# Fused attention and mixture of experts on one core: where the first expert's weights are split into two parts

## The chip, the core and the metric

The kernel runs on one core of a Trainium2 chip. A core has five engines that work side by side, each through its own queue, in order: TensorE (PE in the profile; its weight loads are PEld), VectorE (DVE), ScalarE (ACT), GpSimd (POOL) and SyncE (SP), which here only issues DMA transfers. Tiles lie in SBUF, matmul results in PSUM. The metric is the device time of one execution in microseconds (us).

## The reference

q, k and v have shape [8 batches, 8 heads, 576 rows, 64]. Keys and values are averaged over 8 neighbouring rows, so that each head has 72 of them. Then come softmax attention and a layer of 8 experts in which each of the 4608 tokens goes to the one with the largest logit:

```python
k_p = k.reshape(B, H, Sp, pool, D).mean(axis=3)          # v_p likewise
scores = scale * np.matmul(q, k_p.transpose(0, 1, 3, 2))
attn = softmax(scores); x = np.matmul(attn, v_p)         # -> x [4608, 512]
logits = x @ w_gate;  expert_idx = argmax(logits)        # gate_w: its probability
h = np.maximum(xe @ w1[e], 0.0);  ye = h @ w2[e]         # per expert, w1 512x1024
out[mask] = gate_w[mask, None] * ye
```

All inputs and outputs are float32.

## The kernel before, in words

**Two sections.** `attention` computes x, picks the expert of every token and scatters the rows into a table in DRAM (`dispatched`), sorted by expert. `experts` reads the table back in units of up to 512 rows and multiplies them with the weights of their expert. Between them stands the transition: the last routing, the first matmuls of expert 0, and `plan`, a chain of small VectorE operations that lays out the units. `experts` begins with a critical section (line 728): every engine enters it once the work ahead of it is done.

**Weights in two parts.** TensorE multiplies in a reduced float32 format (fp32r). To keep accuracy, each weight is held as a high part (the cast to fp32r) and a low part (the weight less its high part), in the tile `W` of four planes: w1 high, w1 low, w2 high, w2 low. The weights of one expert come in eight pieces of 128 x 1024 numbers (512 KB): 0 to 3 are w1, 4 to 7 are w2. To split a piece takes a cast on ScalarE (line 424) and a subtraction on VectorE or GpSimd (line 425). The first expert's pieces are loaded (`w_load`, line 418) and split (`w_split`) inside the attention loop, the other experts' in the experts' section.

**The attention loop.** 36 tiles t of 128 rows, four groups of nine, two batches per group. The queues follow the order in which the code is written (no planner moves instructions). In step t: transposes of the probabilities P of tile t on TensorE (line 283) and their copies `pt` out of PSUM on ScalarE (284); scores of tile t+2 (263), their row maxima and the subtraction `sd` on VectorE (267, 270); transposes of q for t+3 (253); at some t a transpose of pooled keys and values of the next group (180) or an expansion of V (207); the exponential of t+2 on ScalarE (276); P times V of tile t (`weigh`, 299); and on VectorE the division by the row sums (311 to 315). Sums of neighbouring rows of k and v (`kv_pool`, 172) run on VectorE, woven in between, and on GpSimd at t = 0 to 2 and then 3, 6, 9, 12, 15 and 18.

**Routing.** Tiles are routed in batches of three (the last two batches have two and one). When a batch is complete, VectorE picks each row's expert (374 to 379, `ro` at 346). In the next step, after `scale`, TensorE counts (356, 359), VectorE reads the counts (361, 362), and GpSimd multiplies (`rp`, 388) and copies the tokens' numbers (384); this falls on every t that is a multiple of 3. A further sum on VectorE (389) needs `rp`; after it GpSimd scatters the three tiles (368, 407). `x_load` (436, 437) at t=29 reads 512 rows of expert 0 back; `x_split` (453 to 456) splits them from t=32 on.

**The first expert's pieces before.** Piece i is loaded in step 18 + i and split in step 21 + i, after everything else of the step: the cast always on ScalarE, the subtraction on GpSimd for i = 0, 3, 6 (t = 21, 24, 27), on VectorE for the other five (t = 22, 23, 25, 26, 28). A piece lies in one of four slots that also take the raw keys and values (`kraw`), so a load waits on SyncE until the slot's last reader is through.

**The transition before.** `multiply` issues the first expert's w1 products for hidden rows 0 to 5 in portions, `hidden(f)` takes row f out of PSUM: a ScalarE activation (468) and a VectorE subtraction (469). `more_hidden` stands inside `plan`, `last_hidden` behind it. The w2 planes are first read after the entry to `experts` (line 882).

**Tiles.** The pooled keys `kTs` have twice the needed columns: each of the two heads that share 128 partitions has its own 72 columns, and the rows of the other head there are zero. Two memsets write the zeros: one on VectorE before anything else (line 101), one on GpSimd (493). The scores read only the 64 rows and 72 columns of their head.

Of the kernel before, what the change touches and what calls it, by code (L numbers as in the profile page):

```python
# [10 lines left out]
F32 = mybir.dt.float32  # L11
# [28 lines left out]
COPIED = 2  # L40
W0T = 21
AHEAD = 8
# [36 lines left out]
def attention(ctx, outer, tc, q, k, v, wg, w1v, w2v, xs, W, cst, carry, tab, banks):  # L79
# [10 lines left out]

    kTs = [one.tile([P, 2, 4, 2 * SK], F32, name=f"kT{i}") for i in range(2)]
    kvp = e1.tile([P, NT, P], F32, name="kvp")
# [7 lines left out]
    nc.vector.memset(kvp, 0.0)  # L100
    nc.vector.memset(kTs[0], 0.0)
    nc.vector.memset(vT, 0.0)
# [73 lines left out]
    def kv_transpose(g, i, bank, what="kv", take=nc.scalar.copy):  # L176


        for c in range(3):
            nc.tensor.transpose(bank[:, c * P : (c + 1) * P], kvp[:, 3 * i + c, :], ident)  # L180
        m = bank[:, 0 : 3 * P].rearrange("p (c bj hp k) -> p hp bj k c", c=3, hp=2, k=8)
        for hp in range(2):
            rk, rv = slice(64 * hp, 64 * hp + 64), slice(64 - 64 * hp, 128 - 64 * hp)
            ko = kTs[g % 2].rearrange("p b j (hp k c) -> p hp (b j) k c", hp=2, c=9)
            vo = vT[:, 0 : 2 * H * KP].rearrange("p (bj hp x) -> p hp bj x", hp=2, x=KP)[:, :, :, 0:SK].rearrange("p hp b (k c) -> p hp b k c", c=9)
            if "k" in what:
                take(out=ko[rk, hp, :, :, 3 * i : 3 * i + 3], in_=m[0:64, hp])
            if "v" in what:
                take(out=vo[rv, hp, :, :, 3 * i : 3 * i + 3], in_=m[64:128, hp])
# [67 lines left out]
    def scores(t):  # L257
        g = t // NT
        for j in range(4):
            for p0, b in [(0, 0), (64, 1)] if KIND(t) == 4 else [(0, parts(t)[0][2]), (64, parts(t)[0][2])]:  # L260
                for hp in range(2):
                    r = slice(64 * hp, 64 * hp + 64)
                    nc.tensor.matmul(pS[p0 : p0 + 64, hp, j * SK : (j + 1) * SK], lhsT=qT[t][r, j * P + p0 : j * P + p0 + 64],  # L263
                                     rhs=kTs[g % 2][r, b, j, hp * SK : (hp + 1) * SK], start=True, stop=True, skip_group_check=True)
        s4 = pS[:, :, 0:288].rearrange("p a (h x) -> p a h x", h=4)
# [149 lines left out]
    def w_load(i):  # L415

        raw = kraw.tile([P, 1024], F32, tag="raw", name=f"w0_{i}")
        nc.sync.dma_start(out=raw.rearrange("p (c f) -> p c f", c=4 if i < 4 else 2), in_=load_piece(w1v, w2v, 0, i))
        w0[i] = raw

    def w_split(i):
        raw = w0.pop(i)
        c, a = slice((i % 4) * 1024, (i % 4 + 1) * 1024), 0 if i < 4 else 2
        nc.scalar.copy(out=W[:, a, c], in_=raw)
        (nc.gpsimd if (W0T + i) % NB == 0 else nc.vector).tensor_tensor(out=W[:, a + 1, c], in0=raw, in1=f32(W[:, a, c]), op=ALU.subtract)

# [15 lines left out]
    def x_open():  # L444
        early.close()
        m1 = outer.enter_context(tc.tile_pool(name="m1", bufs=1, side="right", reuse_waits="tile"))
        u0["H"] = m1.tile([P, 2, 8, 512], F32R, name="H")
        u0["X"] = m1.tile([P, 2, 4, 512], F32R, name="X")

    def x_split(s):  # L450
# [41 lines left out]
    sums()  # L492
    nc.gpsimd.memset(kTs[1], 0.0)

# [48 lines left out]
    for t in range(total):  # L543
# [14 lines left out]
        for at, n, *gj in adds:  # L558
            if at == t:
# [4 lines left out]
                del pieces[third][:n]  # L564
        if 0 <= t - W0T + 3 < 8:
            w_load(t - W0T + 3)
        if 0 < t < total - 2:
# [43 lines left out]
        for bt, (t0, nb) in enumerate(batches):  # L611
            if t == t0 + nb - 1:
                route(bt)
        if 0 <= t - W0T < 8:
            w_split(t - W0T)
        if t == total - 7:
# [23 lines left out]
    def more_hidden():  # L640
        hidden(1)
        multiply(12)

    def last_hidden():
        for f in range(2, AF_EV):
            hidden(f)
            multiply(12)

# [877 lines left out]
```

## Time and profile before

| | |
|---|---|
| median of 3 runs | 631.41 us (631.15 to 631.75) |
| the profiled execution's own time | 627.27 us |
| its span | 625.7 us |
| mean granted clock of TensorE | 0.998 |
| busy: PE, DVE, ACT, POOL | 599.4, 347.9, 241.4, 241.7 us |
| attention loop, transition, entry to the experts | to 171, to 187, at 189 us |
| casts of the first expert's pieces (line 424) | 8, mean 1.04 us |
| subtractions on VectorE and on GpSimd (line 425) | 5 of 1.22 us, 3 of 2.36 us |

The profile is of one execution; its times are microseconds from the span's start. A row of a timeline shows start, duration, engine, line, operation, output <- inputs, and in brackets the idle time before it and what ended it. A row of a group shows busy time and mean duration in ns. A row of waits shows who waited for whom, in total, how often, and the longest. The chain of waits is the work that ended last, followed backwards. A busy TensorE is not TensorE at its peak: its instructions are pipelined, and their ends are modelled.

### The profile page before, as it was taken

The page shows a single profiled execution, that of the slowest core. Times are in us where ns is not written, and L with a number is a line of the kernel's source. Part 1 is how long each engine was busy: PE and PEld are TensorE (multiplying, and loading weights), DVE is VectorE, ACT ScalarE, POOL GpSimd, SP SyncE. Part 2 cuts the span into 40 slices and gives each one's busy share as a digit, 9 for nine tenths or more (in the row PEclk, how much of TensorE's full clock was granted, in tenths as well). Part 3 has the DMA queues.
Part 4 walks back from the last instruction along what each step waited for, and adds up shares of the span by engine and source line. Part 5 has one row for each costly group of instructions (what it writes and reads, how often), then busy time and mean ns, then how long its engine had stood idle before and what let it go on. Part 6 is the DMA issues. An engine that isn't in the chain of part 4 may idle for free.

```text
span 625.7 us, 13480 instructions
## 1 busy us (share of the span) xinstructions
PE 599.4 (96%) x4412; PEld 511.0 (82%) x4412; DVE 347.9 (56%) x731; ACT 241.4 (39%) x453; POOL 241.7 (39%) x288
## 2 busy tenths in 40 slices
PE   6989999999999999999999999999999999999995
PEld 5778989888877878789897888888898888888994
DVE  6699898888751324368475532755137764133220
ACT  2567776877411114065363411523024641021110
POOL 7447657644321122367444411152116861101101
PEclk9999999999999999999999999999999999999999
DMA  9999998982334931506967853064304353100001
GB/s 321 367 279 267 306 262 263 252 253 70 126 111 145 288 112 54 186 25 179 289 185 230 273 115 87 2 211 136 105 35 143 89 146 71 56 0 37 36 4 53
DMA packets 93938, 96.48 MB, mean 154 GB/s; under 512 B 43102, under 2 KB 74846, under 8 KB 93792
## 3 DMA queue, kind: packets, MB, share of 16 engines
q1 hardware_dynamic: 85808, 74.27, 42.3%
q0 software_dynamic: 7440, 20.50, 9.2%
q8 instruction: 61, 1.00, 0.7%
q14 instruction: 85, 0.70, 0.4%
q10 hardware_dynamic: 544, 0.02, 0.0%
HBM read 72.68 MB, written 26.00 MB: 158 GB/s over the span
## 4 chain that ended last, share of the span: by engine, by line
PE 76%; DVE 9%; issue 5%; POOL 4%; ACT 2%; DMA 2%; DVEq 0%; SPq 0%; ACTq 0%; POOLq 0%
PE pU L882 32%; PE pP L860 20%; PE pq L860 10%; PE pU L299 4%; DMA XE<-in_v_dram 2%; PE pP L283 2%; PE pP L463 2%; POOL dispatched L407 2%; PE pS L263 1%; PE pq L253 1%; DVE raw L172 1%; DVE mx L267 1%; POOL raw L172 1%; PE pm L207 1%; DVE xe L315 1%
## 5 line engine op out<-in xcount | busy, mean ns | idle before, releaser
L882 PE MATMUL pU<-W,H 128*128 128x512 f32 x912 | 216.3, 397 | 0.0
L882 PEld LDWEIGHTS pU<-W,H 128*128 128x128 f32 x912 | 171.3, 188 | 41.0
L860 PE MATMUL pP<-X,W 128*128 128x512 f32 (+3 forms) x748 | 143.2, 345 | 4.2 <-DVE W L1069 1.5
L860 PEld LDWEIGHTS pP<-X,W 128*128 128x128 f32 x748 | 122.7, 188 | 21.4 <-issue 3.0
L1351 POOL DMA_INDIRECT out_dram<-Y,GT x51 | 52.8, 1036 | 192.5 <-DVE Y L1174 179.3
L1069 POOL TENSOR_TENSOR W<-ST,W 128x1024 fp32r<-128x1024 f32 x30 | 77.8, 2607 | 88.1 <-ACT W L1061 88.1
L971 ACT ACTIVATE H<-pP 128x512 fp32r<-128x512 f32 (+1 forms) x67 | 36.0, 538 | 191.0 <-PE pP L860 154.7
L1174 DVE TENSOR_SCALAR Y<-pU,GT 128x512 f32<-128x512 f32 x36 | 27.0, 749 | 107.6 <-PE pU L882 106.2
L992 DVE SCALAR_TENSOR_TENSOR H<-pP,H 128x512 fp32r<-128x512 f32 (+2 forms) x73 | 42.2, 580 | 72.0 <-ACT H L971 70.3
L860 PE MATMUL pq<-X,W 128*128 128x512 f32 (+3 forms) x364 | 73.0, 348 | 2.4 <-issue 1.7
L860 PEld LDWEIGHTS pq<-X,W 128*128 128x128 f32 x364 | 60.0, 188 | 11.7 <-issue 2.5
L1061 ACT CAST W<-ST 128x1024 fp32r<-128x1024 f32 x56 | 57.3, 1054 | 6.7 <-DMA ST<-in_moe_w_dram 6.7
L299 PE MATMUL pU<-V,pt 110*128 110x146 f32 (+3 forms) x468 | 56.7, 283 | 1.4 <-ACT pt L284 0.8
L299 PEld LDWEIGHTS pU<-V,pt 110*128 110x128 f32 (+3 forms) x468 | 51.4, 179 | 3.1 <-ACT pt L284 1.8
L407 POOL DMA_INDIRECT dispatched<-xe,ix x36 | 39.8, 1107 | 18.2 <-POOL ix L368 9.8
L971 ACT ACTIVATE H<-pq 128x512 fp32r<-128x512 f32 (+1 forms) x33 | 17.9, 542 | 70.0 <-PE pq L860 68.5
L1069 DVE TENSOR_TENSOR W<-ST,W 128x1024 fp32r<-128x1024 f32 x26 | 40.5, 1560 | 4.6 <-ACT W L1061 4.1
L992 DVE SCALAR_TENSOR_TENSOR H<-pq,H 128x512 fp32r<-128x512 f32 (+2 forms) x35 | 20.8, 595 | 30.6 <-ACT H L971 29.8
L284 ACT COPY pt<-pP 110x384 f32<-110x384 f32 x72 | 30.9, 481 | 6.5 <-PE pP L283 5.8
L1049 DVE TENSOR_TENSOR X<-pS,X 128x512 fp32r<-128x512 f32 x34 | 21.9, 685 | 19.0 <-ACT X L1034 11.3
L276 ACT ACTIVATE P<-sd 128x576 f32<-128x576 f32 x36 | 24.8, 689 | 19.9 <-DVE sd L270 18.0
L172 POOL TENSOR_TENSOR raw<-raw 128x768 f32<-128x768 f32 (+1 forms) x18 | 26.3, 1460 | 13.5 <-DMA raw<-in_v_dram 12.8
(185 smaller groups left out, 625.4 us busy)
## 6 DMA issues: line engine op xcount, KB each, us to landing
ST<-in_moe_w_dram SPq DMA_DIRECT2D x56, 512.0 KB, 6.3
raw<-in_k_dram SPq DMA_DIRECT2D x12, 768.0 KB, 7.3
raw<-in_v_dram SPq DMA_DIRECT2D x11, 768.0 KB, 10.1
XE<-dispatched SPq DMA_DIRECT2D x104, 64.0 KB, 2.5
qa<-in_q_dram SPq DMA_DIRECT2D x24, 256.0 KB, 7.5
w<-in_moe_w_dram SPq DMA_DIRECT2D x8, 512.0 KB, 5.3
XE<-dispatched SPq DMA_DIRECT2D x15, 256.0 KB, 4.3
qa<-in_q_dram SPq DMA_DIRECT2D x2, 1024.0 KB
```

What stands on the lines that cost most here:

```text
L172: return lambda: eng.tensor_tensor(out=out, in0=raw[:, :, 0:n], in1=raw[:, :, n : 2 * n], op=ALU.add)
L284: take(out=pt[t][a][0:R], in_=pPs[a][0:R, 0 : 3 * P])
L299: nc.tensor.matmul(pu[p0 : p0 + n, a, h * VW : (h + m) * VW], lhsT=pt[t][a][0:r, c % 3 * P + p0 : c % 3 * P + p0 + n], rhs=Vs[g % 2][0:r, ...
L407: apart(nc.gpsimd.indirect_dma_start(out=xs, out_offset=bass.IndirectOffsetOnAxis(ap=at, axis=0), in_=rows, in_offset=None))
L860: r = pe.matmul(out=pH[g % 3][:, :m], lhsT=w1s(w, f, k), rhs=x, start=i == 0, stop=i == len(passes) - 1)
L882: r = pe.matmul(out=pY[:, s % 2, :], lhsT=h, rhs=w[:, k * 512 : (k + 1) * 512], start=start and i == 0, stop=stop and i == len(ps) - 1, sk ...
L971: act.activation(out=HH[:, f, o], in_=src[:, o], func=AF.Relu).then_inc(Q["A_h"], 1)
L992: return dve.scalar_tensor_tensor(out=dst[:, f, to], in0=src[:, at], scalar=0.0, in1=f32(HH[:, f, at]), op0=ALU.max, op1=ALU.subtract)
L1061: act.copy(out=(W1H if i < 4 else W2H)[:, o], in_=ST[:, i, :]).then_inc(Q["A_s1" if i < 4 else "A_s2"], 1)
L1069: eng.tensor_tensor(out=(W1L if i < 4 else W2L)[:, o], in0=ST[:, i, :], in1=f32((W1H if i < 4 else W2H)[:, o]), op=ALU.subtract).then_inc( ...
L1174: r = dve.tensor_scalar(out=Y[:, s, :], in0=a, scalar1=gate, scalar2=None, op0=ALU.mult)
L1351: pool.indirect_dma_start(out=out, out_offset=bass.IndirectOffsetOnAxis(ap=GT[:, u, s, 1:2].bitcast(I32), axis=0), in_=Y[:, s, :], in_offs ...
```

## The change

- The pieces 0 to 4 are split at t = 18, 21, 24, 27 and 30, all five subtractions on GpSimd. They are loaded three steps ahead, at t = 15, 18, 21, 24 and 27.
- The pieces 5 to 7 are loaded at t = 32, 33 and 34 into a new tile `late` (12 KB per partition), which lies beside `H` and `X` in the memory that the early pools have given back at t = 31. They are split in the transition: the cast of piece 5 follows hidden row 1 inside `plan`, those of 6 and 7 follow hidden row 2; VectorE subtracts 5 and 6 after hidden row 2 and 7 after hidden row 3.
- The key tiles have half their columns, one set of 72 for both heads of a pair; the two memsets are gone.

```diff
-W0T = 21
+W0T = (18, 21, 24, 27, 30)
@@
-    kTs = [one.tile([P, 2, 4, 2 * SK], F32, name=f"kT{i}") for i in range(2)]
+    kTs = [one.tile([P, 2, 4, SK], F32, name=f"kT{i}") for i in range(2)]
@@
-    nc.vector.memset(kTs[0], 0.0)
@@
-            ko = kTs[g % 2].rearrange("p b j (hp k c) -> p hp (b j) k c", hp=2, c=9)
+            ko = kTs[g % 2].rearrange("p b j (k c) -> p (b j) k c", c=9)
@@
-                take(out=ko[rk, hp, :, :, 3 * i : 3 * i + 3], in_=m[0:64, hp])
+                take(out=ko[rk, :, :, 3 * i : 3 * i + 3], in_=m[0:64, hp])
@@ scores
-                                     rhs=kTs[g % 2][r, b, j, hp * SK : (hp + 1) * SK], ...
+                                     rhs=kTs[g % 2][r, b, j, :], ...
@@ w_load
-        raw = kraw.tile([P, 1024], F32, tag="raw", name=f"w0_{i}")
+        raw = kraw.tile([P, 1024], F32, tag="raw", name=f"w0_{i}") if i < len(W0T) else u0["late"][:, i - len(W0T)]
@@
-    def w_split(i):
-        raw = w0.pop(i)
+    def w_high(i):
+        nc.scalar.copy(out=W[:, 0 if i < 4 else 2, (i % 4) * 1024 : (i % 4 + 1) * 1024], in_=w0[i])
+
+    def w_low(i, eng):
         c, a = slice((i % 4) * 1024, (i % 4 + 1) * 1024), 0 if i < 4 else 2
-        nc.scalar.copy(out=W[:, a, c], in_=raw)
-        (nc.gpsimd if (W0T + i) % NB == 0 else nc.vector).tensor_tensor(out=W[:, a + 1, c], in0=raw, in1=f32(W[:, a, c]), op=ALU.subtract)
+        eng.tensor_tensor(out=W[:, a + 1, c], in0=w0.pop(i), in1=f32(W[:, a, c]), op=ALU.subtract)
@@ x_open
+        u0["late"] = m1.tile([P, 8 - len(W0T), 1024], F32, name="late")
@@
-    nc.gpsimd.memset(kTs[1], 0.0)
@@ the loop
-        if 0 <= t - W0T + 3 < 8:
-            w_load(t - W0T + 3)
+        if t + 3 in W0T:
+            w_load(W0T.index(t + 3))
+        if 32 <= t < 40 - len(W0T):
+            w_load(t - 32 + len(W0T))
@@
-        if 0 <= t - W0T < 8:
-            w_split(t - W0T)
+        if t in W0T:
+            w_high(W0T.index(t))
+            w_low(W0T.index(t), nc.gpsimd)
@@ more_hidden
         hidden(1)
+        w_high(5)
         multiply(12)
@@ last_hidden
             hidden(f)
+            if f == 2:
+                w_high(6)
+                w_high(7)
+            for i in ((5, 6), (7,))[f - 2]:
+                w_low(i, vec)
             multiply(12)
```

More of the change, by code (lines that the diff above doesn't have):

```diff
@@ L263, in scores @@
                     nc.tensor.matmul(pS[p0 : p0 + 64, hp, j * SK : (j + 1) * SK], lhsT=qT[t][r, j * P + p0 : j * P + p0 + 64],
-                                     rhs=kTs[g % 2][r, b, j, hp * SK : (hp + 1) * SK], start=True, stop=True, skip_group_check=True)
+                                     rhs=kTs[g % 2][r, b, j, :], start=True, stop=True, skip_group_check=True)
         s4 = pS[:, :, 0:288].rearrange("p a (h x) -> p a h x", h=4)
```

## The prediction

> **What bounds the kernel now.** First the page: the whole span, and the chain that ended last.
>
> ```profile
> span 625.7 us, 13480 instructions
> PE 76%; DVE 9%; issue 5%; POOL 4%; ACT 2%; DMA 2%; DVEq 0%; SPq 0%; ACTq 0%; POOLq 0%
> w<-in_moe_w_dram SPq DMA_DIRECT2D x8, 512.0 KB, 5.3
> ```
>
> TensorE carries three quarters of the chain, VectorE 9%. The last row is the load of one piece of the first expert's weights: 5.3 us from issue to landing. Where VectorE's share touches this change is seen in the chain between 104 and 172 us (columns: start, duration, engine, tile, line), and the price of a piece in the groups kept apart by shape (busy, mean ns).
>
> ```profile
> 120.40 1.04 ACT W L424
> 121.46 1.23 DVE W L425
> 125.94 1.22 DVE W L425
> 138.73 1.22 DVE W L425
> ...
> L424 ACT CAST W<-w 128x1024 fp32r<-128x1024 f32 x8 | 8.3, 1036 | 0.0
> L425 POOL TENSOR_TENSOR W<-w,W 128x1024 fp32r<-128x1024 f32 x3 | 7.1, 2360 | 0.8 <-ACT W L424 0.8
> L425 DVE TENSOR_TENSOR W<-w,W 128x1024 fp32r<-128x1024 f32 x5 | 6.1, 1220 | 0.7 <-ACT W L424 0.7
> ```
>
> A piece costs a cast of 1.04 us on ScalarE and a subtraction of 1.22 us on VectorE or 2.36 us on GpSimd. Three of the five subtractions on VectorE (tiles t=22, 23, 26) lie on the chain; those of t=25 and 28 do not, nor do the three on GpSimd (t=21, 24, 27). So this change is worth what TensorE loses between tiles 22 and 31, not 5 x 1.22 us.
>
> **What the loop gives back.** TensorE's own order, each row the start of a tile's transposes of P (t=22, 23, 29, 30, 31), and from the chain a key/value transpose and an expansion of V:
>
> ```profile
> 115.24 0.84 PE L283 MATMUL pP<-ident,P 128*110 128x128 f32 x6
> 119.59 0.87 PE L283 MATMUL pP<-ident,P 128*110 128x128 f32 x6
> 126.42 1.71 PE L299 MATMUL pU<-V,pt 110*128 110x146 f32 x12 [0.81 <-ACT pt L284]
> 145.39 0.82 PE L283 MATMUL pP<-ident,P 128*110 128x128 f32 x6
> 148.74 0.82 PE L283 MATMUL pP<-ident,P 128*110 128x128 f32 x6
> 152.26 0.84 PE L283 MATMUL pP<-ident,P 128*110 128x128 f32 x6
> ...
> 110.17 0.33 PE pm L180 x3
> 134.67 0.68 PE pm L207 x6
> ```
>
> Tile 29 has no extra work and takes 148.74 - 145.39 = 3.35 us; tile 30, with a batch's counts, 3.52, so counts cost 0.17. Tiles 22 to 30 take 152.26 - 115.24 = 37.02. Their work is 9 x 3.35, two transposes (0.66), four expansions (2.72), three counts (0.51): 34.04. So 2.98 is lost. Of it tile 22 loses 119.59 - 115.24 - 3.35 - 0.33 = 0.67, before any split on VectorE and beside the cast of t=21, which stays. 2.31 is the most that can come back. The least is the one wait that a row names behind t=23's cast and subtraction, 0.81. I take **2.1**: nearer the upper end, because TensorE sits at its work in tiles 29 and 30, and the casts at t=24 and 27 that stay have an expansion of 0.68 in the following tile beside them, which lets TensorE work while the copies of P wait.
>
> **What the new places cost.** At t=18 GpSimd also adds a chunk of V. Rows of GpSimd, VectorE and TensorE there, and two from the start of the kernel:
>
> ```profile
> 108.92 0.59 POOL L172 TENSOR_TENSOR kvp<-raw 128x192 f32<-128x192 f32 x1
> 117.47 0.22 POOL L388 TENSOR_TENSOR rp<-rp,ro 128x24 f32<-128x24 f32 x1 [3.11 <-DVE rp L361]
> ...
> 111.12 0.95 DVE L172 TENSOR_TENSOR raw<-raw 128x768 f32<-128x768 f32 x1
> 114.74 0.18 DVE L346 TENSOR_TENSOR ro<-rk,rn 128x24 bf16<-128x24 f32 x1
> 115.14 0.18 PE L356 MATMUL pm<-ro,lstrict 128*128 128x24 bf16 x1
> 118.29 0.76 DVE L270 TENSOR_TENSOR sd<-pS,mx 128x576 f32<-128x576 f32 x1
> ...
> 30.20 1.82 POOL L172 TENSOR_TENSOR raw<-raw 128x768 f32<-128x768 f32 x1 [3.24 <-DMA raw<-in_v_dram]
> 30.67 2.17 DVE L172 TENSOR_TENSOR raw<-raw 128x768 f32<-128x768 f32 x1
> ```
>
> The split follows the add at 109.51 and runs to 111.87. Its scatters come 2.36 later; the 3.11 of idle time before the next batch's work covers that (uncovered, VectorE's next sum would wait for `rp`). But VectorE's add at 111.12 now meets it. The last pair shows such a meeting: beside GpSimd's add the same VectorE add took 2.17 instead of 0.95, and ended 0.82 after the other. So this one ends at about 112.7 instead of 112.07. VectorE has no idle time from there to `ro`, which ends at 115.5 to 115.6 instead of 114.92; the counts on TensorE wait for it, at 115.14 before. Cost **0.5** (0 if the add slips by, 0.75 if the whole rest of the split is waited for and no slack is left). The 118.29 row lies inside GpSimd's split of t=21 (117.80 to 120.16) and has its usual 0.76, so not every VectorE instruction waits.
>
> The Trainium skill (SBUF — State Buffer, "Who interferes with whom") draws that line: a VectorE instruction with two SBUF inputs contends with a GpSimd one that reads SBUF, the later one waits until the first is done, and one with a PSUM input doesn't contend. By it the meeting at t=18 is the only one, at 0.75. Were every VectorE instruction held instead, the two pieces new to GpSimd (t=18, 30) would cost up to 2 x 2.36, which the 118.29 row speaks against.
>
> ScalarE's cast at t=18 lies beside an expansion (tile 19), as at t=27: nothing. At t=30 the next tile has none:
>
> ```profile
> 146.57 1.22 DVE L425 TENSOR_TENSOR W<-w,W 128x1024 fp32r<-128x1024 f32 x1
> ...
> 152.87 0.69 ACT L276 ACTIVATE P<-sd 128x576 f32<-128x576 f32 x1 [1.43 <-DVE sd L270]
> 153.57 0.84 ACT L284 COPY pt<-pP 110x384 f32<-110x384 f32 x2
> 154.28 1.48 PE L299 MATMUL pU<-V,pt 110*64 110x146 f32 x24
> 162.01 1.02 POOL L407 DMA_INDIRECT dispatched<-xe,ix  x1 [6.19 <-DVE lh L313]
> ```
>
> The cast of 1.04 goes ahead of the two copies; the first is then done at 154.61 + 0.42 = 155.03, and the matmuls that began at 154.28 wait 0.75. VectorE hands `sd` over some 0.3 earlier, since t=28's subtraction is gone from in front of it: **0.45** (0 to 0.75). GpSimd's part costs nothing there: its scatter waits until 162.01 anyway.
>
> **What is moved behind the loop.** ScalarE, VectorE and TensorE in the transition, SyncE's last load before it, what SyncE waits for at the experts' entry (total, times, longest), and two rows on the order of accesses to W:
>
> ```profile
> 157.28 1.12 SPq L437 DMA_DIRECT2D GT<-dispatched  x1
> 178.90 0.60 ACT L468 ACTIVATE H<-pq 128x512 fp32r<-128x512 f32 x1 [2.20 <-PE pq L463]
> 180.13 0.69 DVE L469 SCALAR_TENSOR_TENSOR H<-pq,H 128x512 fp32r<-128x512 f32 x1
> 182.33 0.69 DVE L469 SCALAR_TENSOR_TENSOR H<-pP,H 128x512 fp32r<-128x512 f32 x1 [1.51 <-ACT H L468]
> 188.76 5.87 PE L860 MATMUL pP<-X,W 128*128 128x512 f32 x24 [1.50 <-DVEq L1400]
> ...
> SPq L728 <- PE pq L463: 4.2, 1, 4.2
> ...
> 143.49 2.36 POOL L425 TENSOR_TENSOR W<-w,W 128x1024 fp32r<-128x1024 f32 x1 [0.40 <-ACT W L424]
> 145.48 1.06 ACT L424 CAST W<-w 128x1024 fp32r<-128x1024 f32 x1
> ```
>
> The three late loads go out behind 158.40, the first lands near 163.7; its cast must be done by hidden row 2 at 178.90, so begin by 177.86: 14 us of cover. The last pair shows ScalarE writing one piece of W while GpSimd still reads another, so a late cast should not wait for the matmuls on the other pieces. The casts of pieces 6 and 7 run from 179.50 to 181.58. VectorE does hidden row 2 until 180.82, two subtractions until 183.26, hidden row 3 until 183.95, the third until 185.17. TensorE ends at 188.76 - 1.50 = 187.26, and the entry waits for it last (4.2 us behind VectorE). 185.17 lies 2.1 us ahead of that: **0**; without that cover, one for one.
>
> The smaller rest also costs 0. The memsets of the key tiles end before data are there:
>
> ```profile
> 5.74 1.55 DVE L172 TENSOR_TENSOR raw<-raw 128x768 f32<-128x768 f32 x2 [0.31 <-DMA raw<-in_k_dram]
> ```
>
> VectorE stands idle 0.31 for the first keys with its memset, and would stand longer without. Scores read the same 72 columns. On SyncE the first piece now goes ahead of a chunk of V and the others further back among the loads of q; no wait of the loop between 80 and 165 us ends with a load, so one piece's 5.3 us at most is absorbed (uncovered, GpSimd's add of V would be late by as much).
>
> **Sum**: -2.1 + 0.5 + 0.45 = -1.15 us. The profiled execution took 627.27 (span 625.7 and 1.6 around it), so 626.1; the runs' median is 631.41, 4.1 above it, and the difference carries over: **630.3**. A difference under 0.2% (1.26 us) cannot be told from none here.
>
> **The rivals.**
> - *Both costs vanish*: the add slips past the split and the cast is covered. Then -2.1 to -2.3, **629.2**. For it: VectorE's earlier hand-over, estimated and not seen. Against: the pair at 30.20.
> - *Nothing is left, the change doesn't pay*: only 0.81 comes back and the costs stand at 0.75 each: +0.7, **632.1**. For it: one wait alone is named. Against: 2.31 us lost in the tiles.
> - *The entry waits for the late splits*. The late tile lies partly where the raw keys and values lay. Suppose its loads are held until 178.9: piece 5 lands at 184.2; its cast (185.24) stands ahead of hidden row 2 on ScalarE (185.84), which stands ahead of VectorE's share (186.53), two subtractions (188.97), hidden row 3 (189.66) and the third subtraction (190.88). The entry comes 3.6 later than at 187.26: +3.6 - 1.15 = +2.45, **633.9**, slower. It decides from a landing of piece 5 at 180.6 on; from 181.7 on the kernel is slower than before. For it: three in-order queues must fit. Against: 14 us of cover, and GpSimd's split of t=30, the last reader of that place, is over some 3 us after its cast.
>
> **How the numbers follow.** Forecast 0.46, costs vanish 0.22, nothing left 0.20, entry 0.12. The forecast's own range is 629.6 to 631.1, so it lies on both sides of the 0.2% line at 630.15: 0.17 of it counts as faster. Faster 0.22 + 0.17 = 0.39, same 0.29 + 0.20 = 0.49, slower 0.12. The range goes from the full 2.3 without costs, less 0.3 for the spread of the runs (628.8), to the second rival (632.2), and leaves out part of the last.
>
> **What would show it.** Tiles 24 to 30 at 3.35 plus their extras, with no wait behind `ro` or ScalarE's copies: the 2.1. A VectorE add of more than 1.5 us beside GpSimd's split at t=18: the 0.5. A wait of TensorE at tile 31 for the copies: the 0.45. At the entry, TensorE still the last that SyncE waits for. Wrong would be a VectorE or DMA wait there, or a gain over 2.3 us.

## The result

| kernel | median | lowest to highest | runs |
|---|---|---|---|
| before | 631.75 us | 631.15 to 634.95 | 5 |
| changed | 637.61 us | 635.00 to 639.06 | 5 |

The ratio is 1.0065 with a 95% interval of 1.0040 to 1.0091: slower, by 0.65% or some 4 us (the medians are 5.9 us apart), where 1.15 us of gain were forecast. The page of the changed kernel's profiled execution (637.93 us), its span and the shares of its chain:

```profile
span 636.3 us, 13472 instructions
...
PE 77%; DVE 7%; issue 6%; POOL 5%; DMA 2%; ACT 1%; DVEq 0%; SPq 0%; ACTq 0%; POOLq 0%
```

VectorE's share of the chain fell from 9% to 7%, as the change means it to; "issue", GpSimd and TensorE have 1% more each, and the span grew by 10.6 us. As will be seen, the two profiled executions belong to two kinds that differ without any change of the kernel, so these two pages must not be subtracted. First the rows that answer the forecast's steps. The transition, on VectorE and TensorE (start, duration, engine, line, operation):

```profile
189.17 2.35 DVE L425 TENSOR_TENSOR W<-late,W 128x1024 fp32r<-128x1024 f32 x2
192.04 1.22 DVE L425 TENSOR_TENSOR W<-late,W 128x1024 fp32r<-128x1024 f32 x1
...
192.74 2.96 PE L462 MATMUL pq<-X,W 128*128 128x512 f32 x12
197.26 1.91 PE L867 MATMUL pP<-X,W 128*128 128x512 f32 x7 [1.56 <-DVEq L1407]
```

The three late subtractions end at 193.26; TensorE ends its hidden rows at 195.70 and begins the experts 1.56 later, against 1.50 before. The moved pieces cost nothing there. Then tile 20 and what follows, GpSimd, VectorE, TensorE and ScalarE:

```profile
113.83 2.36 POOL L425 TENSOR_TENSOR W<-w,W 128x1024 fp32r<-128x1024 f32 x1
117.33 1.03 POOL L406 DMA_INDIRECT dispatched<-xe,ix  x1 [0.28 <-POOL ix L367]
118.84 0.96 POOL L406 DMA_INDIRECT dispatched<-xe,ix  x1 [0.28 <-issue]
...
115.40 1.61 DVE L171 TENSOR_TENSOR raw<-raw 128x768 f32<-128x768 f32 x1
119.50 0.76 DVE L266 TENSOR_REDUCE mx<-pS 128x8 f32<-128x576 f32 x1 [0.61 <-PE pq L252]
...
116.81 0.73 PE L262 MATMUL pS<-kT,qT 64*64 64x72 f32 x32
120.61 0.17 PE L355 MATMUL pm<-ro,lstrict 128*128 128x24 bf16 x1 [0.80 <-DVE mx L266]
...
120.22 0.59 ACT L254 COPY qT<-pq 128x512 f32<-128x512 f32 x1 [2.36 <-PE pU L298]
```

VectorE's add beside GpSimd's split took 1.61, as forecast. But there is something that no row of the kernel before had shown. TensorE's scores end at 117.54, and the maximum over them starts at 119.50, ScalarE's copy of the next q at 120.22 after 2.36 of idle time. TensorE's results were there; the news of them was not. It came while GpSimd went through its scatters (at 117.33, 118.84 and 120.28): for the maximum 1.1 after the first had ended, for the copy 0.4 after the second.

This can be measured over the loop from the trace's semaphore events. TensorE's semaphore is the counter that tells the other engines that a group of matmuls is done. For each group that raises it, take the time from the end of its last matmul to the next raise that the trace records, between 45 and 172 us. In this trace the mean is 0.63 us for the 47 that ended while a scatter ran (longest 2.11), and 0.07 for the 132 others. In the trace of the kernel before that the prediction was made from, it is 0.03 for 54 (longest 0.25) and 0.02 for 130. So two questions were open: is it the chip or the change, and is it what the 4 us went into?

### The profile page after: what moved, and what is told of

It is laid out like the page before. It is cut to its first block, busy times and chain, and to the rows that moved or that the text cites. A ratio compares the mean times of both kernels' runs of the same rounds, so it can differ in the third digit from the quotient of the medians.

```text
span 636.3 us, 13472 instructions
## 1 busy us (share of the span) xinstructions
PE 603.7 (95%) x4412; PEld 513.7 (81%) x4412; DVE 348.9 (55%) x728; ACT 241.5 (38%) x453; POOL 243.4 (38%) x289
## 4 chain that ended last, share of the span: by engine, by line
PE 77%; DVE 7%; issue 6%; POOL 5%; DMA 2%; ACT 1%; DVEq 0%; SPq 0%; ACTq 0%; POOLq 0%
PE pU L889 31%; PE pP L867 21%; PE pq L867 10%; PE pU L298 4%; PE pP L282 2%; POOL dispatched L406 2%; PE pS L262 2%; DMA XE<-in_v_dram 2%; PE pq L252 2%; PE pP L462 2%; PE pm L206 1%; POOL raw L171 1%; DVE mx L266 1%; DVE sd L269 1%; DVE raw L171 1%
## 5 line engine op out<-in xcount | busy, mean ns | idle before, releaser
L867 PE MATMUL pq<-X,W 128*128 128x512 f32 (+3 forms) x364 | 74.5, 353 | 2.5 <-issue 1.9
L1076 DVE TENSOR_TENSOR W<-ST,W 128x1024 fp32r<-128x1024 f32 x26 | 44.2, 1699 | 3.7 <-ACT W L1068 3.1
L406 POOL DMA_INDIRECT dispatched<-xe,ix x36 | 37.2, 1033 | 14.1 <-POOL ix L367 8.2
L266 DVE TENSOR_REDUCE mx<-pS 128x8 f32<-128x576 f32 x36 | 27.1, 754 | 14.5 <-PE pq L252 5.6
```

What stands on the lines that cost most here:

```text
L266: nc.vector.tensor_reduce(out=mx, in_=s4, axis=AX.X, op=ALU.max)
L406: apart(nc.gpsimd.indirect_dma_start(out=xs, out_offset=bass.IndirectOffsetOnAxis(ap=at, axis=0), in_=rows, in_offset=None))
L867: r = pe.matmul(out=pH[g % 3][:, :m], lhsT=w1s(w, f, k), rhs=x, start=i == 0, stop=i == len(passes) - 1)
L1076: eng.tensor_tensor(out=(W1L if i < 4 else W2L)[:, o], in0=ST[:, i, :], in1=f32((W1H if i < 4 else W2H)[:, o]), op=ALU.subtract).then_inc( ...
```

## The experiments

Every job had runs of the kernel before on its own chip; a ratio is always to those. "Experts" is the start of TensorE's first matmul of the experts, "tile n" the start of its transposes of P in that tile. Each traced execution of a job is one of those timed.

**First job: which part of the change?** The changed kernel again (e1), the key tiles alone (e2), the changed kernel with its memsets back (e3), the kernel before without its memsets (e4).

```diff
e2: the kernel before with
-    kTs = [one.tile([P, 2, 4, 2 * SK], ...
+    kTs = [one.tile([P, 2, 4, SK], ...         (and the copies, scores and memsets that go with it)
e3: the changed kernel with
     nc.vector.memset(kvp, 0.0)
+    for _ in range(2):
+        nc.vector.memset(kTs[0], 0.0)
...
     sums()
+    for _ in range(2):
+        nc.gpsimd.memset(kTs[1], 0.0)
e4: the kernel before with
-    nc.vector.memset(kTs[0], 0.0)
-    nc.gpsimd.memset(kTs[1], 0.0)
```

> The changed kernel once more, beside the kernel before on the same chip. Four theories of the loss of 4 us (ratio 1.0065). T1, the moved pieces cost it: the loss comes again, 1.004 to 1.009. T2, the start is at fault (without the memsets of the key tiles TensorE starts 1.4 us earlier and its idle time falls into one stretch of 3.4 us at half clock, at 14.8 to 18.3 us): the loss comes again together with that stretch, and where a run has none of it the time is nearer 632. T3, the slimmer key tiles themselves cost: the loss comes again. T4, it lay with the chip or the recording of the one profiled execution (VectorE and ScalarE there waited 1 to 2 us past TensorE's last scores, which the kernel before never shows): the ratio falls to 0.997 to 1.001, and the profile has no such waits.

> The kernel before with the slimmer key tiles and without their two memsets; the first expert's weights stay where they were. T1 (moved pieces): 631.4, ratio 0.998 to 1.002. T2 (start) and T3 (key tiles): most of the loss, 1.003 to 1.008, with a stretch of half clock near 15 us by T2 and without need of it by T3. T4: 0.998 to 1.002.

> The changed kernel with as much memset work as before put back at the two places (two memsets of the slim tile on VectorE at the start, two on GpSimd behind the sums). T2: the half-clock stretch near 15 us goes, and with it 1.5 to 2 us or more of the loss, so 1.000 to 1.004. T1, T3: as the changed kernel beside it, within 0.1%. T4: as the changed kernel beside it, both near 0.998.

> The kernel before without the two memsets of its wide key tiles, and nothing else. T2: the loss or most of it, 1.003 to 1.008. T1, T3 and T4: 0.998 to 1.002; a gain is not expected, since the first keys arrive 0.31 us after the memset ended.

Measured: 1.0006 (0.9985 to 1.0027), 1.0008 (0.9987 to 1.0029), 0.9996 (0.9973 to 1.0020), 1.0007 (0.9987 to 1.0026), with the kernel before at 626.13. No loss in any of them: T1, T2 and T3 as put fall on this chip, and what is left of them is T4. The kernel before itself is 5.6 us faster here than in the first comparison, without an edit. The key tiles and the memsets are worth nothing that can be measured, as forecast. And the loop does what the prediction said. e1, TensorE and VectorE:

```profile
111.30 0.82 PE L282 MATMUL pP<-ident,P 128*110 128x128 f32 x6
115.18 0.85 PE L282 MATMUL pP<-ident,P 128*110 128x128 f32 x6
150.05 0.85 PE L282 MATMUL pP<-ident,P 128*110 128x128 f32 x6
152.59 1.48 PE L298 MATMUL pU<-V,pt 110*64 110x146 f32 x24 [0.45 <-ACT pt L283]
154.00 0.87 PE L282 MATMUL pP<-ident,P 128*110 128x128 f32 x6
187.17 5.86 PE L867 MATMUL pP<-X,W 128*128 128x512 f32 x24 [1.59 <-DVEq L1407]
...
110.63 1.54 DVE L171 TENSOR_TENSOR raw<-raw 128x768 f32<-128x768 f32 x1
114.84 0.18 DVE L345 TENSOR_TENSOR ro<-rk,rn 128x24 bf16<-128x24 f32 x1
```

**Second job, another chip: the kernel before traced (e5), the changed one (e6), and its two costs taken out (e7), with dummies at the start (e8).** Edits of e7 (e8 has also six more dummy transposes, whose results nobody reads, ahead of `q_transpose(0)`):

```diff
+        if t == 31:
+            w_high(4)                  # the cast, behind tile 31's copies of P
         if 2 < t + 2 < total:
             scores(t + 2)
+        if t == 20:
+            add_halves()               # VectorE's add of V, until now ahead of the scores
...
-        if t in W0T:
-            w_high(W0T.index(t))
-            w_low(W0T.index(t), nc.gpsimd)
+        if t in W0T[:-1]:
+            w_high(W0T.index(t))
+        if t in (*W0T[:-1], 31):
+            w_low(W0T.index(t) if t < 31 else 4, nc.gpsimd)
```

> The kernel before against itself, with its own trace beside those of the changed kernel on the same chip. Its ratio shows what the comparison makes of no change: 0.998 to 1.002. If the prediction's steps hold, its tiles 22 to 30 take 37.0 us again and TensorE begins the experts at 188.2 to 188.8 where no half-clock stretch falls into the start. If the loss of the first comparison lay with the chip (VectorE and ScalarE waiting 1 to 2 us past TensorE's scores), the kernel before shows such waits too wherever the changed one does.

> The changed kernel for a third time. Theory A (the prediction's steps hold, and the loss of the first comparison belonged to the executions measured there): 0.9965 to 1.001 (worked out: -1.15 us, 0.9982), experts begun 1.1 us before the kernel before beside it when neither has a half-clock stretch. Theory B (the change does cost, on some chips): 1.004 or more, with late releases by TensorE in its trace and none in that of the kernel before beside it.

> The changed kernel with its two costs taken out: VectorE's first add of the last chunk of V goes behind the scaling of tile 20 instead of ahead of it, so that it starts after GpSimd's split ended; and the cast of the fifth piece goes behind tile 31's copies of P, its split behind that. If the two costs are what the prediction said (traced in the changed kernel at 0.57 and 0.52 us): VectorE's add takes 0.95 instead of 1.54, TensorE has no wait for the copies at tile 31, and the experts begin 1.1 us earlier than in the changed kernel (186.1 instead of 187.2); time 0.998 of the changed kernel's, 0.9964 of the kernel before's. Rival: the wait for GpSimd's sums (0.56 at tile 22) and the copies of keys stand in instead, and no more than 0.3 us comes back.

> The same with six more dummy transposes of TensorE where it stands idle 1.1 us at 12.4 to 13.5 us, ahead of the first transposes of q. If the half-clock stretch near 15 us comes from TensorE's idle time around 12 us falling into one stretch of 3.4 us, no execution has it: the granted clock is 0.996 or more in every one, and the mean over the runs falls by 1.4 us times the share of executions that had it (half, so 0.7 us); the times spread less. If the stretch comes from elsewhere, clocks and times spread as in the version without.

e5 gave 0.9998 (0.9973 to 1.0022), e6 0.9989 (0.9968 to 1.0010): theory A. e5's rows, to be held against those of e1 (both without a stretch of half clock in the loop):

```profile
111.38 0.82 PE L283 MATMUL pP<-ident,P 128*110 128x128 f32 x6
114.83 0.85 PE L283 MATMUL pP<-ident,P 128*110 128x128 f32 x6
151.85 0.84 PE L283 MATMUL pP<-ident,P 128*110 128x128 f32 x6
155.28 0.86 PE L283 MATMUL pP<-ident,P 128*110 128x128 f32 x6
188.35 5.86 PE L860 MATMUL pP<-X,W 128*128 128x512 f32 x24 [1.50 <-DVEq L1400]
...
110.71 0.95 DVE L172 TENSOR_TENSOR raw<-raw 128x768 f32<-128x768 f32 x1
114.34 0.18 DVE L346 TENSOR_TENSOR ro<-rk,rn 128x24 bf16<-128x24 f32 x1
```

Tile 21 takes 3.88 instead of 3.45, tile 31 takes 3.95 instead of 3.43, and the experts begin 1.18 earlier.

e7 and e8 came out slower, 1.0083 (1.0052 to 1.0114) and 1.0075 (1.0052 to 1.0098), against both theories. The trace of e7 tells a part of why. VectorE's add took 0.95 again, but it had moved from idle time into the row of sums ahead of `ro`, which came at 115.08 instead of 114.84: nothing gained. And the last split had slipped behind the batch's scatters. VectorE, GpSimd, TensorE:

```profile
164.34 2.46 DVE L387 TENSOR_TENSOR rp<-rp,ro 128x24 f32<-128x24 f32 x1
...
164.40 2.35 POOL L425 TENSOR_TENSOR W<-w,W 128x1024 fp32r<-128x1024 f32 x1
...
168.10 3.14 PE L298 MATMUL pU<-V,pt 110*128 110x146 f32 x12 [2.54 <-DVE xe L386]
...
163.62:167.03 3.41, 1.94 (x18) 1.62 (x16) 3.04 (x7) 1.07 (x4) 3.11 (x2) 1.00 0.39 148
167.03:173.86 6.83, 5.76 (x21) 4.92 (x22) 4.32 (x20) 0.22 (x1) 3.50 (x6) 0.50 0.29 111
```

A sum of 24 columns that takes 0.18 elsewhere was held for 2.46, until GpSimd's split ended at 166.75. TensorE then stood idle for 2.54, and the last two rows (a table by stretches: length, then busy us and instructions of TensorE, its weight loads, VectorE, ScalarE and GpSimd, granted clock, DMA share, GB/s) show what that brought on: 3.41 us in which TensorE was busy for 1.94, and after them 6.83 us at half the clock. By the Trainium skill (SBUF — State Buffer, "Who interferes with whom") a VectorE instruction with two SBUF inputs and a GpSimd one that reads SBUF lock each other out until the first is done; the trace agrees with the lock, though by its record the small sum had begun 0.06 ahead and still waited. By the Trainium skill (TensorE: Matmul & The Clock Gate, Part 1, "What's actually happening") the clock is halved after an idle window of about 3.4 us, the windows running freely; the trace agrees with the length, but the window was 0.57 busy, not idle.

This is not the whole loss. The experts begin 2.81 later in e7 than in e5, but the span is 7.25 longer. The other 4.4 lie behind the experts' start, where TensorE stands idle for 2.76 ahead of 224.19 (1.62 at that place in e5) and 3.41 us at half the clock follow. Whether that comes from the held sum is not shown.

**Third job: the costs taken out one at a time.** e9 moves only the cast of piece 4 and keeps its split ahead of the scatters; e10 also splits piece 0 in two halves with a scatter between; e11 adds the six dummies; e12 is the changed kernel.

```diff
e9, in the loop:
+        if t == 31:
+            w_high(len(W0T) - 1)
+            w_low(len(W0T) - 1, nc.gpsimd)
...
-        if t in W0T:
+        if t in W0T[:-1]:
e10: at t = 18
-            w_low(0, nc.gpsimd)
+            w_half(0, 0)               # 512 of 1024 columns; w_half(0, 1) follows that batch's first scatter
e11, at the start:
+    warm(6)
     q_transpose(0)
```

> The changed kernel with one of its two costs taken out: the cast of the fifth piece goes behind tile 31's copies of P on ScalarE, while its split keeps its place on GpSimd, ahead of the scatters (in the earlier version it had slipped behind them, met a VectorE sum there and held it 2.28 us; that is not to come again). If TensorE's wait of 0.45 us at tile 31 is that cast: tile 31 takes 3.44 instead of 3.95 us, the experts begin 0.5 us earlier than in the changed kernel (186.6 to 186.7 against 187.2, without half-clock stretches), no VectorE sum in the tail is held; time 0.999 of the changed kernel's. Rival: the copies of P come late for another reason, and nothing changes.

> The same, and the first piece's split on GpSimd in two halves of 512 columns, the second one behind the first scatter, so that GpSimd is at neither when VectorE's add of the raw values runs (110.6 to 111.5). If the cost at tiles 21 and 22 (0.57 us) is that meeting alone: the add takes 0.95 instead of 1.54, the reciprocal begins at 111.4 instead of 112.1, TensorE's counts at 114.6 instead of 115.1, the experts begin 1.0 to 1.1 us before the changed kernel's (186.1). Rival: GpSimd's later scatters or VectorE's small sums meet the second half instead, and 0.3 us or less comes back.

> The same with six dummy transposes of TensorE at 12.4 to 13.5 us. If the half-clock stretch near 15 us comes from TensorE's idle time ahead of it, no execution has it and the mean falls by about 0.7 us, with fewer executions at a mean clock under 0.996; otherwise clocks and times as without.

> The changed kernel once more beside the kernel before. By the prediction's steps 0.998 (interval about 0.996 to 1.000); if the first comparison's loss is the rule and the two later ones the exception, 1.004 or more, with TensorE's releases coming 1 to 2 us late in its trace.

Measured: 0.9960 (0.9935 to 0.9984), 0.9984 (0.9961 to 1.0007), 0.9951 (0.9931 to 0.9972) and, for the changed kernel, 1.0002 (0.9978 to 1.0027). In e9 the wait at tile 31 is gone (compare 150.05, 152.59 and 154.00 of e1):

```profile
150.26 0.84 PE L282 MATMUL pP<-ident,P 128*110 128x128 f32 x6
152.29 1.48 PE L298 MATMUL pU<-V,pt 110*64 110x146 f32 x24
153.70 0.87 PE L282 MATMUL pP<-ident,P 128*110 128x128 f32 x6
```

Tile 31 takes 3.44 instead of 3.95: the cast's cost is 0.51, and it could be avoided. The times fell by more: e9's mean is 1.8 below e12's (1.5 either way), and what the traces show explains 0.5 of it. e10 gained nothing more; the rival in its expectation had it. VectorE and GpSimd:

```profile
110.61 0.95 DVE L171 TENSOR_TENSOR raw<-raw 128x768 f32<-128x768 f32 x1
113.05 0.78 DVE L377 TENSOR_TENSOR rd<-rg,rm 128x24 f32<-128x24 f32 x1
...
112.49 1.29 POOL L432 TENSOR_TENSOR W<-w,W 128x512 fp32r<-128x512 f32 x1
```

The add is back at 0.95, and a small sum with two SBUF inputs pays 0.78 instead of 0.18 beside the second half, on the same way to `ro`.

The half clock at the start can be seen in e12 and not in e11. The table by stretches, cut where the clock could change (in steps of 3.41 from where full clock began, 4.41 in e12 and 7.25 in e11), e12 first:

```profile
11.24:14.65 3.41, 1.68 (x12) 1.17 (x11) 1.17 (x4) 1.10 (x3) 3.08 (x20) 1.00 1.06 412
14.65:18.06 3.41, 3.26 (x41) 2.79 (x42) 3.32 (x5) 1.20 (x3) 2.15 (x9) 0.50 1.02 378
```

```profile
10.66:14.07 3.41, 2.46 (x21) 1.98 (x20) 1.95 (x5) 1.18 (x3) 3.15 (x17) 1.00 1.06 393
14.07:17.48 3.41, 2.98 (x51) 2.43 (x50) 2.58 (x4) 1.69 (x3) 2.58 (x11) 1.00 1.03 418
```

TensorE is busy 0.49 of the one and 0.72 of the other. Cut in this way, all traces agree: each of the thirteen stretches of half clock that began before 245 us follows a stretch in which TensorE was busy 0.25 to 0.57, and none follows one that was busy 0.58 or more (from 0.49 to 0.57 both happen). Without the dummies the stretch ahead of the scores' first lies between 0.48 and 0.71, by where the steps fall, and six of fifteen traces have half the clock behind it, the kernel before once (e16); none of the five with the dummies has (e8, e11, e14, e15, e18). What it costs is small: e12 is 1.2 us behind e1 at tile 0 and 0.3 from tile 4 on, because ScalarE's wait for VectorE at 34 us, 1.62 in e1, is 0.77 in e12. So T2 is out by its size too. In the times the dummies seem to be worth more: the mean fell by 0.5 from e7 to e8, by 1.7 from e10 to e11 and by 1.1 from e13 to e14 below (1.7, 1.1 and 2.1 either way), clear of noise once. The traces of e10 and e11 are 0.12 apart at the experts' start; only e10's has half the clock again, at 337 us. That the dummies did this is not shown.

**Fourth job, a third chip.** The changed kernel (e13), the same with the six dummies alone (e14), and a version without a piece at tile 18 (e15):

```diff
e15: the changed kernel with e9's lines, the six dummies, and
-W0T = (18, 21, 24, 27, 30)
+W0T = (21, 24, 27, 28, 30)
-            w_low(W0T.index(t), nc.gpsimd)
+            w_low(W0T.index(t), vec if t == 28 else nc.gpsimd)
```

> The changed kernel once more, on whatever chip comes. If the first comparison's loss belongs to one chip and this is not it: 0.997 to 1.001, before at 626 to 628. If it is that chip: before at 631 or more and a ratio of 1.004 or more, with late releases by TensorE in the trace.

> The changed kernel with six dummy transposes of TensorE (0.82 us) in its idle time at 12.4 to 13.5 us, and nothing else changed. If half-clock stretches near 15 us hide the gain: none in the trace, fewer executions under a mean clock of 0.996, the mean 0.5 to 1 us under the changed kernel's beside it, ratio to the kernel before 0.996 to 0.998. If they are not the reason, the same mean as the changed kernel beside it, within 0.4 us.

> The changed kernel with the cast of the last piece in the loop behind tile 31's copies, six dummy transposes at the start, and no piece behind tile 18's sums: the fifth piece of the loop is split on VectorE at tile 28, where the kernel before had one. If the meeting of GpSimd's split and VectorE's add is the cost at tiles 21 and 22: VectorE's add takes 0.95, tile 21 takes 3.46 instead of 3.88 us, 0.57 us come back there and 0.24 are lost at tile 28 (4.30 instead of 4.06 us), so the experts begin 0.3 us earlier than in the version with halves (186.0 or 186.1 at a full clock); time 0.9945 to 0.997 of the kernel before's. Rival: tiles 21 and 22 stay as slow, the cost being something else there; then 0.25 us later than the version with halves.

Here the loss came back: e13 1.0085 (1.0051 to 1.0119), e14 1.0064 (1.0035 to 1.0092), the kernel before at 634.02. e15 is level with it, 1.0009 (0.9984 to 1.0033). All three traces have the late raises: means of 0.67, 0.77 and 0.62 us for those that end beside a scatter, 0.06 to 0.09 for the others. So it goes with the chip, or with something else that changes from job to job: only the chip of e1 was met twice, with prompt raises both times. From here on a chip with prompt raises is called one of the first kind, one with late raises one of the second. e14's ratio can't be told from e13's: the dummies don't take the loss away.

**Fifth job: the kernel before, traced on such a chip (e16).** The chip that came was a fourth one.

> The kernel before, traced. On a chip of the slow kind (before at 631 or more): TensorE's releases that end during a scatter are late there too, by 0.6 to 0.8 us in the mean. If the change loses because its scatters come later and meet more of the scores' releases, the tiles of the kernel before lose 5 to 7 us between tile 3 and 35 against the other chips, where the changed kernel loses 8 to 10, and the difference begins at tile 20 to 22. If the difference lies before tile 18, the moved pieces are not its cause. On a chip of the other kind: 624 to 628, the same trace as before.

The kernel before took 634.78 there (0.9998 to its own other runs, 0.9963 to 1.0034). Its raises beside a scatter are late as well, by 0.45 in the mean over 51. But it pays less for them in the tiles that the change touches. From tile 3 to tile 21, which the change hardly touches, the kernel before loses 4.4 us against the first kind (e16 against e5) and the changed one 3.4 (e13 against e1); from tile 21 to tile 35 they lose 1.1 and 6.6. The same place in both kernels, TensorE's scores in tile 23, GpSimd, VectorE; first e16:

```profile
125.32 0.73 PE L263 MATMUL pS<-kT,qT 64*64 64x72 f32 x32
...
125.67 1.04 POOL L407 DMA_INDIRECT dispatched<-xe,ix  x1 [0.46 <-POOL ix L368]
...
126.37 1.23 DVE L425 TENSOR_TENSOR W<-w,W 128x1024 fp32r<-128x1024 f32 x1 [0.67 <-ACT W L424]
127.52 0.75 DVE L267 TENSOR_REDUCE mx<-pS 128x8 f32<-128x576 f32 x1
...
120.17 0.85 PE L283 MATMUL pP<-ident,P 128*110 128x128 f32 x6
171.00 0.82 PE L283 MATMUL pP<-ident,P 128*110 128x128 f32 x6
194.80 5.87 PE L860 MATMUL pP<-X,W 128*128 128x512 f32 x24 [1.52 <-DVEq L1400]
```

and e13:

```profile
124.98 0.73 PE L262 MATMUL pS<-kT,qT 64*64 64x72 f32 x32
...
125.33 1.03 POOL L406 DMA_INDIRECT dispatched<-xe,ix  x1 [0.45 <-POOL ix L367]
126.84 0.96 POOL L406 DMA_INDIRECT dispatched<-xe,ix  x1 [0.28 <-POOL ix L367]
...
127.49 0.76 DVE L266 TENSOR_REDUCE mx<-pS 128x8 f32<-128x576 f32 x1 [2.13 <-PE pm L179]
140.60 0.76 DVE L266 TENSOR_REDUCE mx<-pS 128x8 f32<-128x576 f32 x1 [2.11 <-PE pm L206]
152.96 0.76 DVE L266 TENSOR_REDUCE mx<-pS 128x8 f32<-128x576 f32 x1 [1.41 <-PE pq L252]
...
173.38 0.82 PE L282 MATMUL pP<-ident,P 128*110 128x128 f32 x6
197.21 5.86 PE L867 MATMUL pP<-X,W 128*128 128x512 f32 x24 [1.56 <-DVEq L1407]
```

In e16 the maximum over the scores starts 1.47 after them, behind VectorE's subtraction. In e13 the subtraction is gone, VectorE stands idle for 2.13, and the maximum starts 1.78 after them. The wait has taken the subtraction's place. Over the loop, 29 of the 33 raises that come more than 0.3 late in e13 have an instruction of another engine that waits for TensorE and starts just then; in e16 it is 16 of 26.

**Sixth job: more scatters (e17), and e15 again (e18).** e17 is the changed kernel with one more scatter behind each of eleven batches, into rows that nothing reads.

```diff
+            if bt < 11:
+                nc.gpsimd.indirect_dma_start(out=cst["spare"], out_offset=..., in_=x[:, 0, :], in_offset=None)
```

> The changed kernel with one more scatter on GpSimd behind each of the first eleven batches' own: the batch's first tile once more, into rows that nothing reads. If a scatter holds TensorE's releases on a chip of the slow kind: there 5 to 11 more late releases between 45 and 172 us (29 before), the new ones arriving 0.5 us after an added scatter ended, and the loop 3 to 10 us longer than the 173.4 us at which tile 35 began on chip 1. If the late releases have another cause, their number and the loop stay (within 1 us). On a chip of the other kind: no late releases and the loop within 1 us of 163.3.

> The version with the last piece's cast behind the copies, six dummy transposes, and the fifth piece of the loop on VectorE at tile 28, again. On a chip of the other kind: 0.994 to 0.997, tile 35 begun at 162.3 to 162.7. On a chip of the slow kind: 0.998 to 1.003 as on chip 1, tile 35 at 171 to 172.

The chip was of the first kind. e17: 1.0001 (0.9977 to 1.0025), raises beside a scatter 0.03 late over 66. More scatters hold nothing there, which leaves the test of the cause on the other kind undone. e18: 0.9982 (0.9955 to 1.0009). Its add takes 0.95, tile 21 3.45 (111.25 to 114.70), and TensorE begins the experts at 186.02, 0.45 before e11: the meeting was the whole cost at tiles 21 and 22, and the piece on VectorE at tile 28 cost nothing, where 0.24 had been expected.

## Why the prediction was wrong

The sum came out on one kind of chip (-1.10 where -1.15 was forecast) and not on the other (+4.32), and the result was measured on the other. There three steps failed: the 2.1 us of the loop did not come back, GpSimd's later scatters were not free, and the 4.1 us between the profiled execution and the median did not carry over.

The later jobs ran on five chips, and every trace is of one of the two kinds: raises of TensorE's semaphore that end beside a scatter are 0.03 to 0.04 us late in the mean (the kernel before as given, e1 to e12, e17, e18: three chips), or 0.45 to 0.77 (the changed kernel of the first comparison, e13 to e16: two chips). On the second kind the kernel before takes 634 to 635 in the median, on the first 626 to 627. What the change did between tile 21 and the experts, changed minus before, from tile starts (columns: e1 - e5 on the first kind, e13 - e16 on the second):

| stretch | first kind | second kind |
|---|---|---|
| tiles 21 and 22 (split at t=18) | +0.58 | +1.57 |
| tiles 23 to 29 (subtractions gone from VectorE) | -2.25 | +0.33 |
| tiles 30 and 31 (cast at t=30) | +0.47 | +1.50 |
| tiles 32 to 34 | +0.01 | +0.89 |
| tile 35 to the experts (transition) | +0.09 | +0.03 |
| sum | -1.10 | +4.32 |

Of the 5.4 us between the columns 2.6 are the loop's gain that did not come back, 1.0 stands behind the split at t=18 and 1.9 in tiles 30 to 34. The first column repeats: e6 and e12 against e5 have sums of -1.14 and -1.09. The second is from one pair of traces on two chips; against the same e16, the changed kernel of the first comparison has +3.11 and e14 +6.79. The spans of e13 and e16 are only 1.3 us apart: e16 had lost 1.91 against e13 ahead of tile 21 and lost 1.1 more behind the experts' start, with a stretch of half clock in each of the two.

- *What the loop gives back*, -2.1: measured -2.25 on the first kind. Right there. On the second kind nothing came back: the step held for VectorE, but the time it freed was not what TensorE waited for; the late raise was.
- *The meeting at t=18*, +0.5: +0.58, through exactly the rows named (add 1.54, `ro`, counts). Right in size, and right in mechanism, since e18, which takes the piece away, gets it back.
- *The cast at t=30*, +0.45: tile 31 lost 0.52, a wait of 0.45 behind the copies. Right, and e9 takes it out.
- *Transition, memsets, SyncE's order*, 0: right on both kinds.
- *GpSimd's scatters come 2.36 later; the 3.11 of idle time before the next batch's work covers that*: this step failed on the second kind. It asked only who waits on GpSimd. In the changed kernel the scatters behind tile 18's split run from 116.08 to 120.0 in e13, over the end of the scores at 116.29; VectorE waits 0.63 for them and ScalarE 2.41 for the next q. At tiles 30 to 34 raises at 153.81 and 168.53 come 2.14 and 1.82 late, against one of 1.90 at 155.13 in e16. The scatters of tile 30 are no later there (from 151.52, 153.04 and 154.48 in e13, from 151.53, 154.09 and 155.54 in e16), so at this place the delay of the scatters is not the cause; which raises they meet differs.
- *The difference of 4.1 us between profiled execution and median carries over*: this is where the failure could have been seen. The profiled execution (627.27) has the time and the prompt raises of the first kind; the three runs (631.15 to 631.75) lie among those of the second (630.5 to 637.9 on e13's chip) and above 107 of the 110 timed in the first three jobs, on the first kind. The three runs have no trace, but by their times the sum was made on a trace of one kind and the result measured on the other. None of the rivals had it; "the entry waits" was the only one that said slower, and its mechanism did not occur.

On the first kind the forecast's 1.15 us can be seen in each pair of traces, but hardly in the times: three comparisons gave 1.0006, 0.9989 and 1.0002, each within some 0.0021. Taken together, the 36 runs of the changed kernel in these jobs have a mean of 626.87 and the 110 of the kernel before 627.24, a difference of 0.37 (about 0.6 either way). Among the runs with a mean granted clock of 0.997 or more it is 0.66 (625.67 over 15, 626.32 over 55; about 0.5 either way). So stretches of half clock may hide a part; where the rest of 1.1 stays is not settled. One place can be named: from the experts' start to the end the traces of the first kind take between 435.6 (e9) and 441.8 us (e8), with waits of TensorE near 220 and 340 us that come out differently in each trace and half the clock behind some of them. That spread is larger than the change.

What was not shown: that the scatter is the cause of the late raise, and not something that goes with it. For it: on the second kind 28 of the 34 raises that came more than 0.3 late in the first changed trace ended beside a scatter, and of the 29 in e13 that came more than 0.5 late, 16 came 0.38 to 0.53 after a scatter's end (the other 13 came 0.95 to 1.52 after one). By the same measure raises of VectorE and ScalarE beside a scatter are late in e13 too, 0.17 over 53 and 0.38 over 28 in the mean, against 0.03 and 0.01 in e1, so it may not be TensorE's alone; but more of their events are missing there. A run that took the scatters away was not made, and e17 fell on the wrong kind. The traces of the second kind also hold fewer semaphore events (7242 to 7304, against 8372 to 8399 in those of the first with the same number of scatters). A missing event alone would not hold up an engine, and the engines did start late; but the recording itself may have a part in it. All timed executions are recorded, and no run here can tell the two apart.

## What to carry to other kernels

Before a sum is made on a trace, check that the trace is of the kind that will be timed: a profiled execution that is 0.7% faster than the median of the runs is a finding, not an offset. When work is moved, follow what comes later because of it (here scatters, by 2.36 us) to everyone it can disturb, and not only to those who wait for its result; and a freed engine gives its time back only if nothing else ends at the same moment. Versions with the cast's cost taken out came out faster on the first kind (e9 0.9960, e11 0.9951; e10 at 0.9984 has 1 inside its interval), and the one run on both (e15, e18) is level on the second and 0.9982 on the first, with 1 inside its interval. The spread between these ratios (0.33%, some 2 us) is larger than that between their starts of the experts (186.02 to 186.86), so the ratios alone don't rank them.

## What the hardware showed that was not expected

- On two chips (and the one of the first comparison) a raise of TensorE's semaphore beside a scatter of GpSimd reaches the waiting engine up to 2.1 us late (2.7 in e14, 2.8 in e15), and on three others it doesn't (0.59 at most, in e6). The places are the same from chip to chip: from tile 11 to tile 20, e13 and e16 run at a fixed distance of 1.9 us.
- A GpSimd subtraction can hold up even a single small sum of VectorE with both inputs in SBUF: 0.18 became 2.46 in e7 and 0.78 in e10, each ending 0.05 behind GpSimd's instruction.
- Every stretch of half clock that was examined came after a stretch of 3.41 us in which TensorE was busy no more than 0.57; it need not have been idle, and such a stretch did not always bring it. In e7 an idle time of 2.5 us in the tail of the loop was followed by 6.8 us of half clock, and the experts began at 191.16, 4.0 after e1's, for 2.28 us of hold.
